# Sparse experts after delta attention and a dense mixture: nine tiles in the first list in place of six, the second list in three pieces

## The chip, the core and the metric

The program runs on one core of one Trainium2 chip. The metric is the device time of one execution in microseconds (us). A core has a matrix engine (TensorE, PE; its weight loads are listed as PEld), three elementwise engines (VectorE, DVE; ScalarE, ACT; GpSimd, POOL) and a queue that only issues transfers (SyncE, SP). Each engine works through its own instruction list in order and waits for the others through semaphores; 16 DMA engines move the data.

## What is computed

Three stages, cut to what matters here:

```python
y   = delta_attention(q, k, v, beta)          # 4 x 8 heads, 768 steps, head_dim 48
x   = y as rows                               # N = 3072 rows, D = 384
x   = sum_e p[:, e] * (relu(x @ w1[e]) @ w2[e])      # dense, E = 4, F = 1024, weights moe_*
# sparse stage, E = 8, F = 1024, weights moe2_*
logits     = (x/|x|) @ (emb/|emb|).T / tau
expert_idx = argmax(logits, axis=1)
gate_w     = softmax(logits)[expert_idx]
for e in range(8):
    mask = expert_idx == e
    out[mask] = gate_w[mask, None] * (relu(x[mask] @ w1[e]) @ w2[e])
```

## The kernel before, in words

**First stage.** The 768 steps are cut into 12 blocks of 64; a block makes 256 rows. Attention for block s+1 runs beside the dense experts of block s, 32 places per block, and the order is written by hand in a table `at`. As soon as a block's dense rows are there, they are routed (`route_pieces`): the row is normalised, its expert is chosen, its place in that expert's list is counted (`rce` holds a running count per expert), the row goes to a DRAM buffer `xb` (L872) and its number to a DRAM table `ids` with 24 tiles of 128 entries for each expert (L873). Beside all that the eight sparse experts' weights are split into pairs of 16-bit halves and written to DRAM as `wimg`.

**Sparse stage.** It works on tiles of up to 128 rows of one expert, numbered here from 0. For each tile POOL gathers the rows from `xb` into `g` (`gather`, L1009, four buffers), SP turns them into `xt` with a transposing transfer (`turn`, L1030), SP loads the expert's weights into one of three slots (`weights`, L1024, four transfers; tile n uses slot n % 3), PE does 72 matmuls for the hidden layer (L1052) and 24 for the output (L1069), ACT and DVE split the hidden layer (L1056, L1057), ACT scales (L1073) and POOL scatters the result (L1074). The loop issues, for tile j: `gather(j + 3)`, `turn(j + 2)`, the tile itself in four steps (hidden 0, hidden 1, output 0, output 1), then `weights(j + 3)`. The four weight transfers are issued with a condition: from tile 3 on they move nothing when tile n has the expert of tile n - 3, since the slot then holds it.

**Lists.** Which expert and which rows a tile has is worked out on the chip. `list_a` (DVE) finds the number of tiles per expert and, for each place of the list, the expert and the row of the table `ids`; it ends with a gather on POOL of these rows into `lsi` (L956). `list_b` turns them with two small matmuls on PE (L965, L966) and makes the row numbers `idx`, the experts `ei` and the flags for the conditional loads. The first list is made while block 11 is still in the dense stage, from the counts of blocks 0 to 10, and takes the first `NA` full tiles in the order of the experts; the second is made after block 11 is routed and takes the rest. `NB = 2 * NS + 7 - NA` places are kept for it. Inside a list the tiles stand in order of the expert, that row is cut into three stretches of about equal length, and place p takes entry p // 3 of stretch p % 3, so that one slot stays with one stretch.

**Order around the change.** While the first tiles run, the last block is routed. `behind` holds what is issued after step 4 * j + n of the tiles: pieces of `route_pieces` at 0, 1, 2, 3, 5, 6, then `list_a(1)` at 7 (after tile 1) and `list_b(1)` at 11 (after tile 2). Tiles 0 to NT - 5 (27 tiles, NT = NA + NB = 31) always run; four more run under two conditions on the number of tiles.

Of the kernel before, what the change touches and what calls it, by code (L numbers as in the profile page):

```python
# [645 lines left out]
class Sparse:  # L646
# [249 lines left out]
        return o  # L896

    def list_a(self, ph):
        nc, rp, cp = self.nc, self.tp, self.tp
        NA = self.NA  # L900
        J = NA if ph == 0 else self.NB
        c = rp.tile([128, 8], F32, name=f"cnt{ph}")
        nc.vector.tensor_tensor(out=c, in0=self.rce, in1=self.e3k, op=ALU.subtract)
        if ph == 0:
            c1 = rp.tile([128, 8], F32, name="cnt1m")
            nc.vector.tensor_scalar(out=c1, in0=c, scalar1=-127.0, scalar2=None, op0=ALU.add)
            nt = self.tiles_of(c1, "ntA", ALU.is_gt, 0)
            cum = self.prefix(nt, "cumA")

            a = self.took = rp.tile([128, 8], F32, name="took")  # L910
            nc.vector.tensor_tensor(out=a, in0=nt, in1=cum, op=ALU.subtract)
            nc.vector.tensor_scalar(out=a, in0=a, scalar1=float(NA), scalar2=0.0, op0=ALU.add, op1=ALU.max)
            nc.vector.tensor_tensor(out=a, in0=a, in1=nt, op=ALU.min)
            nt, cum = a, self.prefix(a, "cumT")
        else:
            nt = self.tiles_of(c, "ntB", ALU.is_gt, 0)
            nc.vector.tensor_tensor(out=nt, in0=nt, in1=self.took, op=ALU.subtract)
            cum = self.prefix(nt, "cumB")


        w = rp.tile([128, 8], F32, name="lsw")
        e = self.lse = rp.tile([128, 1], F32, name="lse")
        k = rp.tile([128, 1], F32, name="lsk")
        l = rp.tile([128, 1], F32, name="lsl")
        sn = rp.tile([128, 2], F32, name="lsn")
        sw = rp.tile([128, 2, 11], F32, name="lsv")
        st, T = self.st, cum[:, 7:8]
        nc.vector.tensor_scalar(out=sw, in0=self.k3.rearrange("p (a b) -> p a b", a=2), scalar1=T, scalar2=None,
                                op0=ALU.is_lt)
        nc.vector.tensor_reduce(out=sn, in_=sw, axis=AX.X, op=ALU.add)  # L930
        nc.vector.scalar_tensor_tensor(out=l, in0=sn[:, 0:1], scalar=st[:, 1:2], in1=st[:, 0:1],
                                       op0=ALU.mult, op1=ALU.add)
        nc.vector.scalar_tensor_tensor(out=l, in0=sn[:, 1:2], scalar=st[:, 2:3], in1=l, op0=ALU.mult, op1=ALU.add)
        nc.vector.tensor_tensor(out=e, in0=self.pidx, in1=T, op=ALU.is_ge)
        nc.vector.scalar_tensor_tensor(out=l, in0=e, scalar=1000.0, in1=l, op0=ALU.mult, op1=ALU.add)
        nc.vector.tensor_scalar(out=w, in0=cum, scalar1=l, scalar2=None, op0=ALU.is_le)
        nc.vector.tensor_reduce(out=e, in_=w, axis=AX.X, op=ALU.add)
        nc.vector.tensor_tensor(out=w, in0=w, in1=nt, op=ALU.mult)
        nc.vector.tensor_reduce(out=k, in_=w, axis=AX.X, op=ALU.add)
        nc.vector.tensor_tensor(out=k, in0=l, in1=k, op=ALU.subtract)  # L940
        nc.vector.tensor_scalar(out=e, in0=e, scalar1=-8.0, scalar2=None, op0=ALU.add)
        if ph == 1:
            nc.vector.tensor_scalar(out=w, in0=self.em8, scalar1=e, scalar2=None, op0=ALU.is_equal)
            nc.vector.tensor_tensor(out=w, in0=w, in1=self.took, op=ALU.mult)
            r = rp.tile([128, 1], F32, name="lsr")
            nc.vector.tensor_reduce(out=r, in_=w, axis=AX.X, op=ALU.add)
            nc.vector.tensor_tensor(out=k, in0=k, in1=r, op=ALU.add)

        nc.vector.scalar_tensor_tensor(out=k, in0=e, scalar=24.0, in1=k, op0=ALU.mult, op1=ALU.add)
        nc.vector.tensor_scalar(out=k, in0=k, scalar1=192.0, scalar2=None, op0=ALU.add)  # L950
        nc.vector.tensor_scalar(out=w[:, 0:1], in0=e, scalar1=0.0, scalar2=1000.0, op0=ALU.is_ge, op1=ALU.mult)
        bi = rp.tile([128, 1], I32, name="lsb")
        nc.vector.tensor_tensor(out=bi, in0=k, in1=w[:, 0:1], op=ALU.max)
        ids = rp.tile([32, 128], F32, name="lsi")
        nc.vector.memset(ids, float(PAD))
        nc.gpsimd.indirect_dma_start(  # L956
            out=ids[0:J], out_offset=None, in_=self.ids,
            in_offset=bass.IndirectOffsetOnAxis(ap=bi[0:J], axis=0), bounds_check=191, oob_is_err=False)
        self.lst = (J, ids, e, cum)
# [120 lines left out]


@with_exitstack
def kernel(ctx, tc, q, k, v, beta, probs, w1, w2, emb, tau, v1, v2, out, NA=6):
    nc = tc.nc
    ctx.enter_context(tc.manual_schedule())
    NS = q.shape[2] // 64
# [4 lines left out]
    sparse = Sparse(ctx, tc, emb, tau, v1, v2, out, NS, ident, pp, NA)  # L1091
# [20 lines left out]
    second = {o: [g for p, g in steps[1][0] if p == o] for o in range(-8, 0)}  # L1112
# [31 lines left out]
    at = defaultdict(list)  # L1144
# [38 lines left out]
    lists, tiles, cols = {}, {}, {}  # L1183
# [27 lines left out]

    last = 32 * (NS - 1)
    at[last + 1].append(opened)
    at[last + 12].append(lambda: sparse.list_a(0))
    at[last + 18].append(phase_a)
    at[last + 30].append(lambda: columns(0))

# [21 lines left out]
    behind = defaultdict(list)  # L1239
    for o, g in zip((0, 1, 2, 3, 5, 6), pieces):  # L1240
        behind[o].append(g)
    behind[7].append(lambda: sparse.list_a(1))
    behind[11].append(lambda: lists.__setitem__("B", sparse.list_b(1)))

    def tile(j, ahead):
        C = cols.pop(j)
# [62 lines left out]
```

## Time and profile before

| what | value |
|---|---|
| three runs, median (lowest, highest) | 1208.43 us (1207.02, 1209.62) |
| the profiled execution, own time | 1208.76 us |
| its span | 1207.0 us |
| PE busy | 1134.7 us (94%) |
| DVE busy | 772.6 us (64%) |
| ACT busy | 636.6 us (53%) |
| POOL busy | 366.4 us (30%) |
| mean granted clock of PE | 0.973 |

Busy time is the time with an instruction of that engine running; waits are what is left. In the rows further down a window line gives, for a stretch in us from the span's start, the busy time of PE, PEld, DVE, ACT and POOL with the number of instructions, then PE's granted clock as a share of full speed (1.00 is 2.4 GHz, 0.50 is 1.2 GHz), the mean busy share of the 16 DMA engines and the GB/s they moved. A timeline line gives start, duration, engine, source line, operation, output<-input, and in brackets the idle time of the engine before it and what ended it.

### The profile page before, as it was taken

The numbers are of one execution on the slowest core, as the hardware profiler recorded it, in microseconds if no ns is written. First come the engines' busy times: TensorE is split into PE (matmuls) and PEld (weight loads), VectorE is DVE, ScalarE is ACT, GpSimd is POOL, SyncE is SP. The second block draws the span as 40 slices with busy tenths as digits, with TensorE's granted clock in tenths as the row PEclk, the third lists the DMA queues.
The fourth block names the chain that finished last, engine by engine and source line by source line (L and its number), as shares of the span: only waits on it lengthen the run. The fifth ranks groups of instructions, "written<-read, shape, count | busy, mean of one in ns | idle before, by whom it ended". The sixth has DMA issues, their size and how long they took to land. (4 is left out here: it accounts for less than half of the span.)

```text
span 1207.0 us, 34016 instructions
## 1 busy us (share of the span) xinstructions
PE 1134.7 (94%) x13738; PEld 891.1 (74%) x13738; DVE 772.6 (64%) x2818; ACT 636.6 (53%) x1167; POOL 366.4 (30%) x346
## 2 busy tenths in 40 slices
PE   2359899999999999999999999999999999999997
PEld 2337677778777777777777778777777777888776
DVE  8858668788687786877868778687863543211221
ACT  8668766565565655656566565665653141222222
POOL 4346533231322313232133322332411203222221
PEclk8579999999999999999999999999999999999999
DMA  9971155645836556364474554646421293978951
GB/s 175 214 160 41 28 93 132 120 93 133 113 100 121 90 133 113 100 121 91 133 106 132 122 118 132 106 133 120 106 80 28 71 323 88 354 197 261 319 144 30
DMA packets 246162, 159.17 MB, mean 132 GB/s; under 512 B 195231, under 2 KB 229356, under 8 KB 246000
## 3 DMA queue, kind: packets, MB, share of 16 engines
q1 hardware_dynamic: 241600, 147.26, 53.1%
q0 software_dynamic: 4400, 9.68, 2.6%
q8 instruction: 110, 1.80, 0.7%
q14 instruction: 52, 0.43, 0.2%
HBM read 142.53 MB, written 35.80 MB: 148 GB/s over the span
## 5 line engine op out<-in xcount | busy, mean ns | idle before, releaser
L621 PE MATMUL po<-W,H 128*128 128x384 f16 x2304 | 408.6, 327 | 11.6 <-DVE H L604 8.8
L599 PE MATMUL ph<-xT,W 128*128 128x256 f16 x3456 | 411.2, 274 | 0.2
L599 PEld LDWEIGHTS <-W 128*128 128x128 f16 x3456 | 333.3, 98 | 49.6 <-issue 0.7
L621 PEld LDWEIGHTS <-H 128*128 128x128 f16 x2304 | 220.2, 98 | 146.6 <-DVE H L604 14.5
L604 DVE SCALAR_TENSOR_TENSOR H<-ph,H 128x512 f16<-128x512 f32 x192 | 131.7, 687 | 181.6 <-ACT H L603 180.2
L603 ACT ACTIVATE H<-ph 128x512 f16<-128x512 f32 x192 | 113.7, 593 | 143.3 <-PE ph L599 142.1
L788 POOL TENSOR_TENSOR wso<-wst,wso 128x768 f16<-128x768 f32 x64 | 105.6, 1650 | 245.4 <-ACT wst L787 237.5
L1057 DVE SCALAR_TENSOR_TENSOR H<-ph,H 128x512 f16<-128x512 f32 x54 | 37.2, 690 | 152.7 <-ACT H L1056 152.7
L1052 PEld LDWEIGHTS <-slot 128*128 128x128 f16 x1944 | 112.3, 99 | 3.8 <-issue 0.5
L1052 PE MATMUL ph<-xt,slot 128*128 128x128 f16 x1944 | 114.7, 221 | 0.1
L334 DVE TENSOR_TENSOR tt<-tt,pr 128x60 f32<-128x60 f32 (+34 forms) x660 | 111.0, 210 | 0.7
L1069 PE MATMUL po<-slot,H 128*128 128x384 f16 x648 | 110.0, 326 | 0.6 <-DVE H L1057 0.6
L330 DVE TENSOR_TENSOR pr<-tt,KQ 128x60 f32<-128x60 f32 (+34 forms) x660 | 108.8, 203 | 0.8
L1069 PEld LDWEIGHTS <-H 128*128 128x128 f16 x648 | 62.1, 98 | 39.1 <-DVE H L1057 0.9
L1074 POOL DMA_INDIRECT out_dram<-ob,idx x27 | 27.4, 1013 | 168.4 <-ACT ob L1073 112.0
L786 ACT ACTIVATE wso<-wst 128x768 f16<-128x768 f32 x64 | 53.4, 835 | 42.5 <-issue 24.3
L1056 ACT ACTIVATE H<-ph 128x512 f16<-128x512 f32 x54 | 32.2, 597 | 79.3 <-PE ph L1052 76.4
L293 POOL TENSOR_TENSOR AO<-G,AO 32x256 f16<-32x256 f32 x48 | 32.7, 680 | 97.5 <-ACT AO L292 95.6
L873 POOL DMA_INDIRECT ids<-idt,si x24 | 24.7, 1028 | 118.8 <-DMA ids<-idt,si 60.0
L359 PEld LDWEIGHTS <-TB 128*128 128x128 f16 x1152 | 34.4, 98 | 35.5 <-ACT TB L351 27.7
L587 POOL TENSOR_TENSOR W<-W,W 128x768 f16<-128x768 f32 x29 | 47.7, 1654 | 37.7 <-ACT W L586 28.5
L1073 ACT ACTIVATE ob<-po,sm 128x384 f32<-128x384 f32 x27 | 15.7, 580 | 82.1 <-PE po L1069 82.0
(261 smaller groups left out, 1444.3 us busy)
## 6 DMA issues: line engine op xcount, KB each, us to landing
slot<-wimg SPq DMA_DIRECT2D x108, 768.0 KB
wst<-in_moe_w_dram SPq DMA_DIRECT2D x65, 384.0 KB
wimg<-wso SPq DMA_DIRECT2D x64, 384.0 KB
W<-in_moe_w_dram SPq DMA_DIRECT2D x15, 384.0 KB
xb<-xr SPq DMA_DIRECT2D x48, 98.0 KB
Kr<-in_k_dram SPq DMA_DIRECT2D x24, 192.0 KB
Qr<-in_q_dram SPq DMA_DIRECT2D x24, 192.0 KB
Vr<-in_v_dram SPq DMA_DIRECT2D x24, 192.0 KB
```

What stands on the lines that cost most here:

```text
L330: nc.vector.tensor_tensor(out=p, in0=t[:, :, j:j + 1].to_broadcast([128, m, j]), in1=AT[:, j, 0:j].unsqueeze(1).to_broadcast([128, m, j]), ...
L334: nc.vector.tensor_tensor(out=t, in0=t, in1=p, op=ALU.subtract)
L587: low.tensor_tensor(out=lo, in0=t, in1=hi, op=ALU.subtract)
L599: nc.tensor.matmul(ph[:, i], w1[:, a, k, 128 * i:128 * i + 128], xT[:, b, k], start=(n == 0), stop=(n == 8))
L603: nc.scalar.activation(out=H[:, 0], in_=ph, func=AF.Relu)
L604: nc.vector.scalar_tensor_tensor(out=H[:, 1], in0=ph, scalar=0.0, in1=H[:, 0], op0=ALU.max, op1=ALU.subtract)
L621: nc.tensor.matmul(po[t], H[:, a, i, 128 * t:128 * t + 128], w2[:, b, i], start=(f == 0 and i == 0 and n == 0), stop=(f == 3 and i == 1 an ...
L786: self.nc.scalar.activation(out=o[:, 0], in_=t, func=AF.Copy, scale=scale)
L788: self.nc.gpsimd.tensor_tensor(out=o[:, 1], in0=t, in1=o[:, 0], op=ALU.subtract)
L1052: nc.tensor.matmul(ph[:, i], w[:, a, k, 128 * (i % 2):128 * (i % 2) + 128], xt[:, 3 * b + k], start=(m == 0), stop=(m == 8))
L1057: nc.vector.scalar_tensor_tensor(out=H[:, 1], in0=ph, scalar=0.0, in1=H[:, 0], op0=ALU.max, op1=ALU.subtract)
L1069: nc.tensor.matmul(po, H[:, a, i], w[:, b, i % 2], start=(q == 0 and i == 0 and m == 0), stop=(q == 1 and i == 3 and m == 2))
```

## The change

The first list takes nine full tiles in place of six, so the second has 22 places in place of 25. `list_a` becomes a generator with two `yield`s; the first list still runs through it in one go, the second is made in three pieces, after steps 7, 9 and 11, and `list_b(1)` comes after step 18 in place of 11.

```diff
     def list_a(self, ph):
...
             nt = self.tiles_of(c, "ntB", ALU.is_gt, 0)
             nc.vector.tensor_tensor(out=nt, in0=nt, in1=self.took, op=ALU.subtract)
             cum = self.prefix(nt, "cumB")
+        yield
...
         nc.vector.tensor_tensor(out=k, in0=l, in1=k, op=ALU.subtract)
         nc.vector.tensor_scalar(out=e, in0=e, scalar1=-8.0, scalar2=None, op0=ALU.add)
+        yield
         if ph == 1:
...
-def tile_delta_attention__then__two_moes_kernel(ctx, tc, q, k, v, beta, probs, w1, w2, emb, tau, v1, v2, out, NA=6):
+def tile_delta_attention__then__two_moes_kernel(ctx, tc, q, k, v, beta, probs, w1, w2, emb, tau, v1, v2, out, NA=9):
...
-    at[last + 12].append(lambda: sparse.list_a(0))
+    at[last + 12].append(lambda: list(sparse.list_a(0)))
...
-    behind[7].append(lambda: sparse.list_a(1))
-    behind[11].append(lambda: lists.__setitem__("B", sparse.list_b(1)))
+    second = sparse.list_a(1)
+    for o in (7, 9, 11):
+        behind[o].append(lambda: next(second, None))
+    behind[18].append(lambda: lists.__setitem__("B", sparse.list_b(1)))
```

PE, around the two small matmuls of the second list (`lsi`, `lse`). Before, between the last output matmul of tile 2 and the first hidden one of tile 3:

```order
L1069 LDWEIGHTS H_17459
L1069 MATMUL po<-slot_3_16251,H_17459 128x384
L965 MATMUL ps<-id_16252,lsi 128x32
L966 MATMUL ps<-id_16252,lse 1x32
L1052 LDWEIGHTS slot_0_16240
L1052 MATMUL ph<-xt_17171,slot_0_16240 128x128
```

Now, between the two halves of tile 4's output:

```order
L1072 LDWEIGHTS H_17703
L1072 MATMUL po<-slot_1_16245,H_17703 128x384
L968 MATMUL ps<-id_16252,lsi 128x32
L969 MATMUL ps<-id_16252,lse 1x32
L1072 LDWEIGHTS H_17743
L1072 MATMUL po<-slot_2_16246,H_17743 128x384
```

They stand seven half tiles later in PE's list.

POOL, in the first tiles: `g` is a tile's gather, `out_dram` a tile's scatter, `lsi` the gather of the list. Before:

```order
L873 DMA ids<-idt,si 24576x1 x2
L1074 DMA out_dram<-ob,idx_16685 3072x384
L956 DMA lsi<-ids,lsb 25x128
L1009 DMA g_16256<-xb,idx_16685 128x392
L1074 DMA out_dram<-ob,idx_16685 3072x384
L1009 DMA g_16257<-xb,idx_17500 128x392
```

Now:

```order
L873 DMA ids<-idt,si 24576x1 x2
L1077 DMA out_dram<-ob,idx_16685 3072x384
L1012 DMA g_16256<-xb,idx_16685 128x392
L1077 DMA out_dram<-ob,idx_16685 3072x384
L959 DMA lsi<-ids,lsb 22x128
L1012 DMA g_16257<-xb,idx_16685 128x392
```

The gather of tile 5 and the scatter of tile 2 now stand ahead of the list's gather, and tile 6 takes its rows from the first list (`idx_16685`).

DVE, at the two cuts of the second list in the change (H is the hidden layer of a tile, two instructions a tile):

```order
L886 TENSOR_REDUCE cumB<-pfw 128x8
L1060 SCALAR_TENSOR_TENSOR H_17386<-ph,H_17386 128x512
L1060 SCALAR_TENSOR_TENSOR H_17426<-ph,H_17426 128x512
L930 TENSOR_SCALAR lsv<-k_221,cumB 128x22
...
L943 TENSOR_SCALAR lse<-lse 128x1
L1042 TENSOR_SCALAR sm<-sm 128x1
L1043 RECIPROCAL sm<-sm 128x1
L946 TENSOR_SCALAR lsw<-em_210,lse 128x8
```

Before, the 27 instructions from `cnt` to the clearing of `lsi` (L903 to L955) stood in one row ahead of both H instructions of tile 2.

## Rows read from the trace of the kernel before

**Rows 1.** Timeline of PE: the first hidden matmuls of tiles 1, 2, 4 and 5

```profile
989.13 4.18 PE L1052 MATMUL ph<-xt,slot 128*128 128x128 f16 x72
997.17 4.18 PE L1052 MATMUL ph<-xt,slot 128*128 128x128 f16 x72
...
1018.07 4.18 PE L1052 MATMUL ph<-xt,slot 128*128 128x128 f16 x72
...
1025.99 4.18 PE L1052 MATMUL ph<-xt,slot 128*128 128x128 f16 x72
```

**Rows 2.** Timeline of all engines from tile 2's output to tile 3

```profile
1001.57 1.21 DVE L1057 SCALAR_TENSOR_TENSOR H<-ph,H 128x512 f16<-128x512 f32 x2
...
1002.24 3.75 PE L1069 MATMUL po<-slot,H 128*128 128x384 f16 x22 [0.56 <-DVE H L1057]
...
1005.97 1.04 POOL L956 DMA_INDIRECT lsi<-ids,lsb  x1 [4.46 <-DMA slot<-wimg]
...
1008.35 0.24 PE L965 MATMUL ps<-id,lsi 32*128 32x32 f32 x1 [2.36 <-DMA lsi<-ids,lsb]
...
1008.56 5.78 PE L1052 MATMUL ph<-xt,slot 128*128 128x128 f16 x72
```

**Rows 3.** Windows: the stretch right behind that wait

```profile
1008.00:1012.00 4.00, 3.65 (x36) 3.58 (x37) 1.36 (x9) 0.00 (x0) 2.42 (x3) 0.57 0.49 118
```

**Rows 4.** DMA view from 985 us on: issues, size of one, of the weights

```profile
slot<-wimg SPq DMA_DIRECT2D x96, 768.0 KB
```

**Rows 5.** Timeline of SP: weight loads of tiles 0, 4, 7; turn of tile 7

```profile
960.17 2.24 SPq L1024 DMA_DIRECT2D slot<-wimg  x4
...
1000.58 1.48 SPq L1024 DMA_DIRECT2D slot<-wimg  x4
...
1023.26 3.26 SPq L1024 DMA_DIRECT2D slot<-wimg  x4
1026.63 1.44 SPq L1030 DMA_TRANSPOSE xt<-g  x1
```

**Rows 6.** Windows: starts of two loads, and the three transposes behind loads 7 to 9

```profile
962.00:962.50 0.50, 0.50 (x5) 0.30 (x4) 0.04 (x1) 0.00 (x0) 0.38 (x1) 1.00 0.86 307
...
1025.00:1025.50 0.50, 0.50 (x5) 0.29 (x3) 0.00 (x0) 0.00 (x0) 0.00 (x0) 1.00 0.83 270
...
1034.50:1035.00 0.50, 0.50 (x13) 0.50 (x11) 0.00 (x0) 0.19 (x1) 0.00 (x0) 1.00 1.29 65
1035.00:1035.50 0.50, 0.50 (x13) 0.50 (x11) 0.00 (x0) 0.00 (x0) 0.00 (x0) 1.00 0.06 19
...
1045.00:1045.50 0.50, 0.50 (x13) 0.50 (x11) 0.37 (x1) 0.00 (x0) 0.42 (x1) 1.00 1.49 61
...
1055.50:1056.00 0.50, 0.50 (x5) 0.29 (x3) 0.05 (x1) 0.00 (x0) 0.00 (x0) 1.00 2.52 34
1056.00:1056.50 0.50, 0.50 (x5) 0.29 (x3) 0.00 (x0) 0.00 (x0) 0.00 (x0) 1.00 0.06 25
```

**Rows 7.** Windows: start of load 16, and the transpose behind load 18

```profile
1097.00:1097.50 0.50, 0.50 (x5) 0.31 (x4) 0.00 (x0) 0.00 (x0) 0.00 (x0) 1.00 0.83 344
...
1126.50:1127.00 0.50, 0.50 (x5) 0.31 (x4) 0.47 (x3) 0.00 (x0) 0.07 (x1) 1.00 1.74 92
```

**Rows 8.** Windows: end of a transposing transfer in the first stage

```profile
390.75:391.00 0.25, 0.25 (x5) 0.23 (x3) 0.00 (x0) 0.00 (x0) 0.00 (x0) 1.00 3.51 95
```

**Rows 9.** Timeline of DVE: what waited for that transfer

```profile
391.16 0.76 DVE L249 TENSOR_TENSOR KQ<-KTB 128x512 f16<-128x512 f16 x2 [1.82 <-DMA KTB<-KB]
```

**Rows 10.** Windows: PE's idle time in block 0, with the clock

```profile
125.00:126.00 1.00, 0.52 (x4) 0.10 (x1) 0.97 (x2) 0.97 (x2) 0.00 (x0) 1.00 0.00 0
126.00:127.00 1.00, 0.22 (x2) 0.11 (x2) 0.97 (x2) 0.98 (x2) 0.00 (x0) 1.00 0.00 0
127.00:128.00 1.00, 0.73 (x22) 0.64 (x23) 0.61 (x2) 0.97 (x3) 0.00 (x0) 1.00 0.00 0
```

**Rows 11.** Windows: a load alone on the queue

```profile
1040.00:1044.00 4.00, 4.00 (x52) 3.24 (x50) 0.00 (x0) 0.58 (x1) 0.24 (x1) 1.00 1.03 418
```

More of the change, by code (lines that the diff above doesn't have):

```diff
@@ L1082, with kernel @@
 @with_exitstack
-def kernel(ctx, tc, q, k, v, beta, probs, w1, w2, emb, tau, v1, v2, out, NA=6):
+def kernel(ctx, tc, q, k, v, beta, probs, w1, w2, emb, tau, v1, v2, out, NA=9):
     nc = tc.nc
```

## The prediction

> **What bounds the kernel now.** I read the busy times first: PE has 1134.7 of 1207.0 us, so only PE's gaps and its clock can give time back. In the sparse stage the timeline of PE shows tiles that follow each other without a gap: tile 4 starts at 1018.07 and tile 5 at 1025.99, so an undisturbed tile costs 7.92 us [rows 1]. The stage's one large gap is where the second list is made [rows 2]: PE stands 0.56 us inside tile 2 because its H came late from DVE, which was busy with the list; then 2.36 us ahead of the list's small matmuls, which wait for `lsi`, issued by POOL at 1005.97. Behind that gap the windows give a clock of 0.57 between 1008 and 1012 us [rows 3], the lower level (1.2 GHz) for most of it, and tile 3's 72 hidden matmuls take 5.78 us in place of 4.18 [rows 1, 2]. In a last view, the windows in steps of half a us, I look at the DMA engines, because the change also alters which tiles share weights; there the reader is to see that a tile's transpose runs only when the load issued ahead of it has ended.
>
> **What goes: the list's gap.** The small matmuls now stand inside tile 4. POOL can issue `lsi` once tile 2 has been scattered, at about 1007.5; in the old order it took 1008.35 - 1005.97 = 2.4 us from issue to PE [rows 2], so it is there by 1010, and PE reaches the matmuls at about 1019: nine us of cover. The gap and the lost clock go: 2.36 + (5.78 - 4.18) = 3.96 us. The cut of the list puts both H instructions of tile 2 ahead of the second piece, so the 0.56 us goes too. Together **-4.52 us**. The 0.2 us of the small matmuls stays. What the list now delays: on POOL the gather of tile 6 stands behind `lsi`, on SP `turn(6)` waits for that gather; tile 6 starts at about 1029, some 20 us after, so this costs nothing. DVE's third piece stands ahead of tile 3's H, but runs while tile 3's hidden matmuls do. Three more columns in the first list's small instructions cost nothing either: DVE's list instructions work on one row there, and the list is not made later.
>
> **What comes: two more loads, in longer rows.** Counting the reference's choices for its inputs gives 631, 338, 180, 721, 242, 603, 98, 259 rows for experts 0 to 7, and 4, 2, 1, 5, 1, 4, 0, 1 full tiles after eleven blocks. Put through the list's rule, the tiles' experts are, with NA = 6: 0 0 1 0 0 1 | 0 3 5 1 3 5 2 3 5 2 4 6 3 4 7 3 5 7 3 5 7, and with NA = 9: 0 0 2 0 1 3 0 1 3 | 0 3 5 1 4 5 2 4 6 3 5 7 3 5 7 3 5 7. 27 tiles run in both. A load moves data when the expert differs from that three places earlier: before for tiles 0, 1, 2, 7, 8, 9, 12, 16, 17, 18, 20, 22; now for 0, 1, 2, **4, 5**, **10, 11, 12, 13**, 15, **17, 18, 19, 20**. The longest row behind the start grows from three to four, and there is a new pair at tiles 4 and 5, early.
>
> A load is 4 x 768 KB [rows 4]. The queue of SP works in order: tile 7's turn was issued at 1026.63 [rows 5] but the transpose's burst of DMA activity ends at 1035.0, right behind load 7; those of tiles 8 and 9 end at 1045.5 and 1056.0 [rows 6]. Load 7 began to flow at 1025.0, so a cycle (load, the other tiles' gather and scatter beside it, transpose, and the nearly empty half us after it) takes 10.0, 10.5, 10.5 us. The second row, loads 16 to 18, flows from 1097.0 and its last burst ends at 1127.0 [rows 7]: 30.0 / 3 = 10.0. Call the cycle c; it lies between **10.0 and 10.5**, I take 10.2, the mean of all six. A tile takes 7.92, so each load in a row makes the next `xt` 2.3 us later against PE, and a row that lasts long enough runs out of lead. From the end of a transpose's burst to a waiting engine I take 0.5 us: in the first stage a transpose's burst ended at about 391.0 and DVE, which waited for it, began at 391.16 [rows 8, 9]; 0.5 leaves room for the windows' half us.
>
> - **Tile 13** (and **tile 20**, the same): load 10 flows 6.9 us after tile 7's start (1025.0 - 1018.07 for load 7 and tile 4 [rows 1, 6]), so tile 13's `xt` is there 6.9 + 4c + 0.5 after it, and PE wants it after 6 x 7.92 = 47.5. Late by 4c - 40.1: nothing at c = 10.0, **0.7 us** at 10.2, 1.9 at 10.5. Tile 12's comes 38.0 after, wanted at 39.6: in time.
> - **Tile 5**: load 4's issue at 1000.58 [rows 5] stays, since it stands behind the routing of the last block; before, it moved nothing. A load flows 1.7 to 1.8 us after its issue (960.17 to 962.0, 1023.26 to 1025.0 [rows 5, 6]), so at 1002.4; tile 5's `xt` is there at 1002.4 + 2c + 0.5 = 1023.3. PE without the old gap ends tile 2 at 1005.43 (1002.24 + 3.75 - 0.56), then two tiles and 0.2: 1021.5. **1.8 us** late; 1.4 at c = 10.0, 2.4 at 10.5. Tile 4's `xt`, at 1013.1, is wanted at 1013.35: in time.
>
> The clock after these new gaps is not in the trace. From below, 1.53 us idle within three us of block 0 left it at 1.00 [rows 10]; from above, 2.36 us in one piece lost it for 1.60 us of PE time [rows 2, 3]. 1.8 is nearer to 1.53, 0.7 far below: I charge nothing, and keep 1.6 us per gap for the upper end.
>
> Sum: -4.52 + 1.8 + 0.7 + 0.7 = **-1.3 us**. Against the profiled execution's own time of 1208.76 that is 1207.5; that execution lies 0.33 us above the median of the runs, so 1208.43 - 1.3 = **1207.1**. A measurement of this kernel can tell about 0.2%, 2.4 us, from no change: my forecast is no change that can be told.
>
> **Rivals.** (a) *The queue keeps up.* With c at 10.0 or under, tiles 13 and 20 wait for nothing and tile 5 for 1.4 us or less: -3.1, or 1205.3; with c under 9.3 tile 5 waits for nothing either: -4.5, or 1203.9. For it: the second row of three did run at 10.0, and a load alone moves 418 GB/s [rows 11], which is 7.5 us for its bytes. Against it: the emptier half us behind each transpose [rows 6], and 10.5 twice. The Trainium skill (DMA: Bandwidth & Descriptors, section Bandwidth) gives 436 GB/s as the ceiling and, in the section Latency and other measured facts, 261 GB/s for a DMA transpose; as an estimate from that page a cycle would be 3.54 MB / 436 + 0.2 MB / 261 = 8.9 us, no gap would be left at tiles 5, 13 and 20, and the time would be 1203.9. The trace's 10.0 to 10.5 disagrees, and the measurement decides the sum.
>
> (b) *The new gaps cost the clock.* At c = 10.5 tile 5's gap is 2.4 us, as long as the old one, and takes 1.6 us of clock with it, at the very place that was to be cured; tiles 13 and 20 wait 1.9 each. -4.5 + 2.4 + 1.6 + 3.8 = +3.3: 1211.7, and 1214.9 if those two lose the clock as well. It decides from a gap of about 2 us on. For it: two of three cycles in the first row, and a 2.36 us gap that did lose it. Against it: the mean cycle is shorter.
>
> (c) *The small matmuls wait again*, at their new place: only if `lsi` came nine us late; I give it no chance of its own.
>
> **How the numbers follow.** Forecast 0.41, (a) 0.33, (b) 0.26. The forecast's own span, 1205.5 to 1210.5, lies nearly all within 0.2%; (a) counts as faster but for a little at its edge, (b) as slower but for a little. So faster 0.35, same 0.40, slower 0.25. The range takes (a) whole and (b) up to where a second gap loses the clock: 1203.8 to 1213.0.
>
> **What would show it.** Right: no idle time of PE ahead of the two small matmuls, none inside tile 2, tile 3's 72 matmuls in 4.18 us; PE idle just ahead of the first hidden matmul of tile 5 (about 1.8 us), 13 and 20 (under 1 us each), each with a transpose's burst ending half a us earlier; a clock of 1.00 through the stage. Wrong: no gap at tile 5 (then (a)), a clock of 0.5 behind one of the gaps (then (b)), a gap at other tiles, or loads for other tiles than those listed.

## The result and the profile after

The changed kernel takes **1226.67 us** (median of 4 runs, 1222.40 to 1228.22) where the kernel before takes 1209.03 on the same chip (4 runs): a ratio of **1.0143, interval 1.0123 to 1.0163**. It is slower by some 17.6 us, where no change that can be told was forecast, and it lies outside the range. The profiled execution has a span of 1226.4 us against 1207.0.

The timeline of PE in the changed kernel, first hidden matmuls (L1055) of tiles 1, 2, 3, 4, then the list's two small matmuls, then tiles 5, 6, 11, 12, 13 and 20. The columns are start, duration, engine, line, operation, tiles; in brackets how long PE stood before it and for what.

```profile
988.69 4.18 PE L1055 MATMUL ph<-xt,slot 128*128 128x128 f16 x72
996.93 4.18 PE L1055 MATMUL ph<-xt,slot 128*128 128x128 f16 x72
1004.85 4.18 PE L1055 MATMUL ph<-xt,slot 128*128 128x128 f16 x72
1018.64 5.69 PE L1055 MATMUL ph<-xt,slot 128*128 128x128 f16 x72 [5.71 <-DMA xt<-g]
1026.21 0.24 PE L968 MATMUL ps<-id,lsi 32*128 32x32 f32 x1
1026.30 0.19 PE L969 MATMUL ps<-id,lse 32*1 32x32 f32 x1
1030.17 4.18 PE L1055 MATMUL ph<-xt,slot 128*128 128x128 f16 x72 [1.62 <-DMA xt<-g]
1038.10 4.35 PE L1055 MATMUL ph<-xt,slot 128*128 128x128 f16 x72
...
1078.47 4.18 PE L1055 MATMUL ph<-xt,slot 128*128 128x128 f16 x72
...
1087.72 4.18 PE L1055 MATMUL ph<-xt,slot 128*128 128x128 f16 x72 [0.71 <-DMA xt<-g]
...
1099.62 5.81 PE L1055 MATMUL ph<-xt,slot 128*128 128x128 f16 x72 [3.47 <-DMA xt<-g]
...
1162.19 5.60 PE L1055 MATMUL ph<-xt,slot 128*128 128x128 f16 x72 [4.83 <-DMA xt<-g]
```

What the change was made of has come: no idle time stands ahead of the small matmuls at 1026.21, tile 3 runs its 72 matmuls in 4.18 us, and PE's two idle times of [rows 2] are gone. In their place PE waits for `xt` at five tiles. The waits of PE from 975 us on (total, times, longest):

```profile
PE ph L1055 <- DMA xt<-g: 16.3, 5, 5.7
PE po L1072 <- DVE sm L1042: 0.6, 3, 0.2
```

The tally against before: -4.52 us for the list's gap, +16.34 for the five waits (5.71 + 1.62 + 0.71 + 3.47 + 4.83), +0.6 for `sm`, and +4.56 for the clock at tiles 4, 13 and 20 (5.69 + 5.81 + 5.60 in place of 3 x 4.18). That is 17.0 of the 19.4 us between the spans; the rest is spread, for instance tiles 5 to 11 begin 48.30 / 6 = 8.05 us apart in place of 7.92. The forecast had three waits of 3.2 us in sum and nothing for the clock. The list of loads in the prediction is confirmed by the bytes: two loads more are 2 x 4 x 786,432 bytes = 6.29 MB, and the pages of before and after read

```profile
DMA packets 246162, 159.17 MB, mean 132 GB/s; under 512 B 195231, under 2 KB 229356, under 8 KB 246000
```

```profile
DMA packets 247314, 165.46 MB, mean 135 GB/s; under 512 B 195352, under 2 KB 229488, under 8 KB 247152
```

Now the places that answer to [rows 5] and [rows 6]. SP's timeline, the issue of load 4 and of tile 4's transpose:

```profile
1000.75 3.80 SPq L1027 DMA_DIRECT2D slot<-wimg  x4
1004.59 3.71 SPq L1033 DMA_TRANSPOSE xt<-g  x1
```

Windows of the changed kernel: the start of load 4, the transposes behind loads 4 and 11 and, in full, behind load 12, and the 4 us behind tile 13's start. The columns are the stretch, its length, busy time of PE, PEld, DVE, ACT and POOL, the granted clock, the DMA share and GB/s.

```profile
1006.50:1007.00 0.50, 0.50 (x13) 0.50 (x11) 0.10 (x1) 0.00 (x0) 0.50 (x1) 1.00 0.35 49
1007.00:1007.50 0.50, 0.50 (x13) 0.50 (x11) 0.00 (x0) 0.02 (x1) 0.18 (x1) 1.00 0.82 307
...
1015.50:1016.00 0.50, 0.00 (x0) 0.00 (x0) 0.00 (x0) 0.00 (x0) 0.50 (x1) 0.50 3.82 125
...
1073.50:1074.00 0.50, 0.50 (x13) 0.50 (x10) 0.47 (x1) 0.00 (x0) 0.20 (x2) 1.00 4.43 169
...
1084.50:1085.00 0.50, 0.48 (x3) 0.09 (x2) 0.50 (x1) 0.12 (x2) 0.00 (x0) 1.00 3.60 104
1085.00:1085.50 0.50, 0.29 (x2) 0.21 (x3) 0.38 (x3) 0.00 (x0) 0.00 (x0) 1.00 0.09 37
1085.50:1086.00 0.50, 0.50 (x5) 0.29 (x3) 0.00 (x0) 0.00 (x0) 0.00 (x0) 1.00 0.05 10
1086.00:1086.50 0.50, 0.50 (x5) 0.29 (x3) 0.00 (x0) 0.00 (x0) 0.00 (x0) 1.00 1.07 325
...
1087.50:1088.00 0.50, 0.28 (x6) 0.31 (x7) 0.00 (x0) 0.12 (x1) 0.00 (x0) 1.00 1.04 424
...
1095.50:1096.00 0.50, 0.50 (x5) 0.20 (x2) 0.00 (x0) 0.00 (x0) 0.00 (x0) 1.00 3.38 270
...
1100.00:1104.00 4.00, 4.00 (x46) 4.00 (x44) 0.36 (x1) 0.60 (x1) 1.28 (x2) 0.57 1.01 408
```

The reader is to see three things. Load 4 was issued at 1000.75, but flows only from 1007.0 (by the packet records its first packets begin at 1002.7 and are held for up to 4.3 us each; see the last section). The burst behind load 12 (share 3.60, few GB/s) ends at 1085.0, and tile 12 starts at 1087.72, 2.7 us later; behind load 4 it is 1016.0 and 1018.64, behind load 13 1096.0 and 1099.62. And after the burst behind load 12 the DMA engines stand nearly still for a us (0.09, 0.05), with load 13 already on the queue; in the half us after 1016.0 and 1096.0 the share was 0.34 and 0.67.

The trace's records of single DMA packets tell why the burst is not the end. Packets of SP's queue that began in each half us, behind load 12:

```
half us from   256-byte packets (transpose)   6144-byte packets (loads)
1083.5                    0                           38
1084.0                  348                            1
1084.5                  155                            2
1085.0                    0                            3
1085.5                   20                            0
1086.0                  239                           15
1086.5                    6                           16
1087.0                    0                           10
1087.5                    0                           26
```

The transpose of a tile is 768 packets of 256 bytes (128 x 6 x 256 = 196,608 bytes) and moves here in two parts, some 500 and some 260, with 1 to 1.5 us of pause between them. The burst is the first part. The next load begins to move only with the second. This shape belongs to the place in a row and not to the transpose: by the same records those of tiles 4, 6 and 11 of the kernel before, with no load moving ahead of them, ran whole in 1.1 us, where those of tiles 7, 8 and 9 took 2.4 to 2.8 us.

### The profile page after: what moved, and what is told of

It reads as the page before. It is cut to its first block, busy times and chain, and to the rows that moved or that the text cites. A ratio compares the mean times of both kernels' runs of the same rounds, so it can differ in the third digit from the quotient of the medians.

```text
span 1226.4 us, 34016 instructions
## 1 busy us (share of the span) xinstructions
PE 1140.2 (93%) x13738; PEld 893.4 (73%) x13738; DVE 774.3 (63%) x2818; ACT 636.9 (52%) x1167; POOL 367.1 (30%) x346
## 5 line engine op out<-in xcount | busy, mean ns | idle before, releaser
L1055 PE MATMUL ph<-xt,slot 128*128 128x128 f16 x1944 | 118.2, 223 | 16.4 <-DMA xt<-g 16.3
L1055 PEld LDWEIGHTS <-slot 128*128 128x128 f16 x1944 | 115.2, 100 | 21.3 <-issue 18.1
```

The source lines that it names most:

```text
L1055: nc.tensor.matmul(ph[:, i], w[:, a, k, 128 * (i % 2):128 * (i % 2) + 128], xt[:, 3 * b + k], start=(m == 0), stop=(m == 8))
```

## The experiments

Fourteen kernels, each timed beside the kernel before on its chip. The medians of the kernel before there:

| experiments | before, us |
|---|---|
| nine tiles in the old places; six in the new; nine without the later loads; transpose ahead of its load | 1210.05 |
| a row of four; the gather a tile earlier; ScalarE's queue; without scatters | 1209.09 |
| rows cut; without the transposes of the rows; the first of the last four | 1208.63 |
| the second, third and last of the last four | 1208.17, 1212.77, 1211.24 |

The ratio to before and its 95% interval are those on record for the runs; they lie up to 0.2% from the quotient of the two medians. Theory A: a transpose stands behind its tile's load on SP's queue, and the list of nine puts loads in rows. Theory B: the new places of the list's pieces make the waits. Theories C and D put it on the loads' bytes, or on gathers and scatters.

### Nine tiles, old places

```
- tile_delta_attention__then__two_moes_kernel(..., NA=6):
+ tile_delta_attention__then__two_moes_kernel(..., NA=9):     # the rest as before
```

> Only the size of the first list is changed (nine), the second list's pieces stay where the kernel before has them. Theory A (a tile's DMA transpose stands behind that tile's weight load in SP's queue, and the list of nine puts the loads in rows of two and four): TensorE waits for xt at tiles 4, 5, 12, 13 and 20 as in the changed kernel (16.3 us in 5 waits there), and the list gap ahead of tile 3 is back, so 1226.4 + 2 to 4.5 = 1228 to 1231 us. Theory B (the new places of the list's pieces, which move work of VectorE, GpSimd and the ids' gather, make the waits): about the kernel before, 1207 to 1211 us.

Measured 1226.37 us, 1.0150 (1.0117 to 1.0184). The waits of PE:

```profile
PE ph L1052 <- DMA xt<-g: 9.4, 3, 4.5
PE ps L965 <- DMA lsi<-ids,lsb: 6.7, 1, 6.7
PE po L1069 <- DVE H L1057: 0.7, 1, 0.7
```

The size alone makes the kernel as slow as the changed one, and a little less slow than the 1228 to 1231 expected. The three `xt` waits stand at tiles 12, 13 and 20 (1.59, 3.34, 4.46); at tiles 4 and 5, against the expectation, there is none: PE stood 6.7 us for the list just before. Part of this loss is thus the list's, whose `lsi`, issued at 1006.02, let PE go on at 1011.43, 5.4 us later in place of 2.4; load 4 flowed beside it. That load 4 is the reason is not shown.

### Six tiles, new places

```
  NA=6
- behind[7]: list_a(1), whole             + behind[7], [8], [9]: its three pieces
```

> Six tiles in the first list as before, and the second list in three pieces at places 7, 8 and 9 with its small matmuls at 11 as before. Theory A: no new wait for xt, 1205 to 1210 us, at most the 0.56 us wait of the second matmuls changes. Theory B: waits for xt appear, 1215 us or more.

Measured 1210.35 us, 1.0008 (0.9989 to 1.0027). The waits view has one line for PE, the list's 3.9 us, and none for `xt`: theory B falls, though the time lies 0.35 us above theory A's span.

### Nine tiles without the later loads

```
- kw = dict(cond=cv > 0, cond_hint=False)
+ kw = dict(cond=cv > 1, cond_hint=False)     # never true; from tile 3 on no weights come
```

> The changed kernel with the condition of every weight load behind the first three never true: it leaves out the weights of the tiles from the fourth on, so that what remains is the gain of the change with no load in the way. Theory A: no wait for xt of over 0.5 us, all tiles at 7.92 to 8.1 us, and the kernel before less the list gap, its clock and the H wait: 1209.0 - 4.5 = 1203 to 1206 us. Theory B: the waits stay, 1220 us or more.

Measured 1204.67 us, 0.9958 (0.9941 to 0.9974): 5.1 us less than before, and PE waits for nothing in the whole stage. The gain of 4.5 us is real; the loads take it back.

### Rows cut

```
+ kw = dict(cond=cv > (1 if n in (4, 12, 19) else 0), cond_hint=False)
```

> The changed kernel with the loads of places 4, 12 and 19 left out (their tiles use the weights that lie in the slot): eight loads behind the first three remain, the longest row is two (10, 11 and 17, 18). Theory A (rows): no wait for xt of over 0.5 us is left and the clock stays, 1203 to 1207 us. Rival (each load costs something wherever it stands, 20 us over eleven loads): eight of them cost about 14 us, 1216 us or more.

Measured 1204.49 us, 0.9963 (0.9947 to 0.9978), and again no wait of PE. Eight loads leave the gain whole, eleven cost 22 us more. At one price a load the eight would have cost about 14 us, so what counts is which loads follow one another. It also shows that load 5 alone, with no load 4 ahead, is in time.

### A row of four in the kernel before

```
- if n >= 3:
+ if n >= 3 and n != 10:          # NA=6; load 10 runs unconditionally
```

> The kernel before with one load more: place 10 is loaded whether its expert differs or not, which makes the row 7, 8, 9 a row of four and changes nothing else. Theory A: xt waits at tile 10 by 2.5 to 4 us, about 1.5 us of clock with it, and tile 9 waits 0.3 us as before: ratio 1.003 to 1.005, 1213 to 1216 us where before is 1210. Theory E (the row is harmless, and the waits of the changed kernel come from its list's other order of tiles or from load 4): within 1 us of before.

PE's timeline at tile 10:

```profile
1070.35 5.81 PE L1052 MATMUL ph<-xt,slot 128*128 128x128 f16 x72 [3.77 <-DMA xt<-g]
```

3.77 us of wait (theory A's upper end is 4) and 5.81 - 4.18 = 1.63 of clock, in a list that is otherwise the old one; at tile 9 PE's record shows no wait. The trace is for theory A. The times do not settle it: 1213.61 us, 1.0017 (0.9991 to 1.0044), runs from 1208.34 to 1215.25.

### The transpose ahead of its load

```
-     if j + 2 < sure: turn(j + 2)
      tile(j, sure)
      if j + 3 < sure:
+         turn(j + 3)
          weights(j + 3)
```

> The changed kernel with one line moved: each tile's transpose is issued ahead of that tile's weight load and not behind it (the first three likewise). Theory A: the waits for xt (16.3 us and 4.6 us of clock) are gone, 1204 to 1208 us, unless a load is now late. Theory C (two more loads of 3.1 MB and their rows are too much for the DMA engines, whichever goes first): TensorE waits for the slots' weights in place of xt, 1215 to 1228 us.

Measured 1220.57 us, 1.0081 (1.0044 to 1.0118). PE's waits, SP's longest wait between 1005 and 1018 us, and its timeline at load 5:

```profile
PE ph L1055 <- DMA slot<-wimg: 13.0, 15, 2.3
```

```profile
SPq L1033 <- DMA g<-xb,idx: 9.2, 1, 9.2
```

```profile
1014.51 1.29 SPq L1033 DMA_TRANSPOSE xt<-g  x1
1017.59 1.67 SPq L1027 DMA_DIRECT2D slot<-wimg  x2
```

Every wait for `xt` is gone, tile 4 starts without any, and now the loads are late (theory C's sign). One reason is in the other two fences: SP stood at tile 5's transpose for 9.2 us until its gather had landed, and issued load 5 another 3.1 us later, 11.6 us after tile 2 had left the slot at 1006.0.

### The same with the gather a tile earlier

```
-     if j + 3 < sure: gather(j + 3)
+     if j + 4 < sure: gather(j + 4)
```

> As the run with the transpose ahead of the load, and each tile's gather one tile earlier, so that SP's queue does not stand at a transpose that waits for its gather (there turn 5 waited until 1014.51 and load 5 was issued at 1017.59 in place of about 1007). Theory A (order on SP's queue is what costs): tile 5 in time, and the last of a row of four late by the cycle alone, 4 x 10 us against 39.6: 0 to 3 us at tiles 13 and 20 each; 1205 to 1212 us. Theory D (the gathers and scatters, which run between and beside the loads, slow each load whatever the order is): waits for slots of 10 us or more stay, 1215 to 1221 us.

Measured 1216.27 us, 1.0055 (1.0032 to 1.0079): the time lies in theory D's span, and the waits for slots are just under its 10 us.

```profile
PE ph L1055 <- DMA slot<-wimg: 9.6, 10, 2.0
```

Tiles 4 and 5 wait 2.1 us each for their weights, so tile 5 is not in time, though theory A had it so. The longest wait is at tile 13, inside its hidden matmuls; the 18 behind it, 1.18 us at full clock, show the clock's fall:

```profile
1095.26 2.10 PE L1055 MATMUL ph<-xt,slot 128*128 128x128 f16 x18 [1.96 <-DMA slot<-wimg]
```

### Transposes on ScalarE's queue

```
- self.nc.sync.dma_start_transpose(...)
+ self.nc.scalar.dma_start_transpose(...)
```

> The changed kernel with the tiles' transposes issued by ScalarE in place of SP, so that they stand in another queue than the loads. Theory A: waits for xt of over 1 us are gone, and the loads follow each other without a transpose between them; 1204 to 1210 us. Theory D (transposes, gathers and loads share the DMA engines, and order in one queue is not what delays them): xt still waits 10 us or more in sum, 1218 us or more.

Measured 1270.52 us, 1.0491 (1.0431 to 1.0550): as theory D has it, and worse. ScalarE's timeline (tile 10's transpose, tile 11's, and the H behind that), then PE's at tile 10:

```profile
1064.67 1.52 ACTq L1033 DMA_TRANSPOSE xt<-g  x1
...
1080.21 1.23 ACTq L1033 DMA_TRANSPOSE xt<-g  x1
1081.54 0.60 ACT L1059 ACTIVATE H<-ph 128x512 f16<-128x512 f32 x1 [8.45 <-issue]
```

```profile
1091.58 5.81 PE L1055 MATMUL ph<-xt,slot 128*128 128x128 f16 x72 [3.40 <-DMA xt<-g]
```

Tile 10's transpose was issued at 1064.67 and ended the wait at 1091.58, 26.9 us later, though no load stood ahead of it in its queue; in the changed kernel tile 12's, behind its load, took from 1073.05 to 1087.72, 14.7 us. And ScalarE, which stood at a transpose whose gather was late (tile 11's gather, issued at 1066.76, let it go on at 1080.21), kept PE waiting for H for 23.3 us in sum. So "behind the load on the same queue" is not the whole mechanism: beside loads that are under way, in a queue of its own, this transpose fared worse. The Trainium skill says that spreading DMAs over SP, ACT and GpSimd does not help bandwidth, since they all run on the same 16 DMA engines (DMA: Bandwidth & Descriptors, section Rules for kernel authors); the trace agrees that there is no gain, and shows a loss besides, 26.9 us against 14.7.

### Without scatters

```
  ob = ...; nc.scalar.activation(out=ob, in_=po, ...)
- nc.gpsimd.indirect_dma_start(out=self.out, ...)      # tiles 1 to 20
```

> The changed kernel without the scatter of the output of tiles 1 to 20 (their rows of the output are left out). Theory A: the loads' cycle is set by load and transpose, so the waits for xt stay within 3 us of 16.3 in sum, 1222 us or more. Theory D: the scatters, which share the DMA engines and GpSimd's queue with the gathers, are a large part of the delay: the waits fall under 10 us, 1216 us or less.

Measured 1219.46 us, 1.0089 (1.0065 to 1.0113), between the two again.

```profile
PE ph L1055 <- DMA xt<-g: 12.2, 4, 6.4
```

Tile 13 waits 2.09 us in place of 3.47, tile 20 2.21 in place of 4.83, tiles 5 and 12 not at all; tile 4 waits 6.38, and tile 19, which had not waited, 1.55. The scatters are a part of the cycle: without them the waits are a quarter shorter, and tiles 13 and 20 keep the clock.

### Without the transposes of the rows

```
+ if n in (5, 11, 12, 13, 18, 19, 20): return (*T, self.xt)    # the xt of the tile before
  xt = self.xt = self.t2.tile(...)
```

> The changed kernel with the transposes of tiles 5, 11 to 13 and 18 to 20 left out (they compute with the xt of the tile before), so that the rows are loads alone with their gathers and scatters. Theory A1 (the transposes in a row both wait and hold the load behind them): the load cycle falls from 10 to about 8.5 us, waits for slots at tiles 12, 13, 20 under 1 us each; tile 4 waits as before (5.7 us and clock), 1212 to 1216 us. Theory C (3.1 MB a tile with gather and scatter is too much): the cycle stays at 10 us and slots wait 2 us or more at tiles 13 and 20, 1218 us or more.

Measured 1211.74 us, 1.0014 (0.9993 to 1.0035). PE waits once, 5.1 us at tile 4. A window over loads 11 to 13:

```profile
1061.50:1087.00 25.50, 25.50 (x323) 20.85 (x321) 5.51 (x13) 6.49 (x16) 7.66 (x8) 1.00 1.02 410
```

The loads with their gathers and scatters flow at 410 GB/s without a break; by the packet records loads 12 and 13 begin 8.4 and 8.5 us after the one before. No slot is late: theory C falls for rows of four without transposes. With a transpose in each cycle the bursts of the changed kernel end at 1063.0, 1074.0, 1085.0 and 1096.0: 11.0 us.

### A version with the gain and without the loss

Of the next four kernels three keep six tiles in the first list, hence the old loads, and take the list off PE's front by making its small matmuls in tile 3 and gathering tile 6 late. The last kernel goes back to nine.

```
  NA=6; list_a(1) in pieces at 7, 9, 10
+ behind[14]: list_b(1)
+ in tile j == 4: gather(6) ahead of gather(7)
```

> Six tiles in the first list, so the loads of the kernel before, but the second list in pieces at 7, 9 and 10, its small matmuls at 14 and the gather of tile 6 one tile later, so that nothing of the list stands at TensorE's front. Theory A (the gain is the list gap with its clock and the H wait; the loss is rows of loads): all of the gain, none of the loss: 1203 to 1206 us where before is 1209, ratio 0.995 to 0.997. Rival: turn 6 now waits on SP for its late gather and holds load 7 behind it: a wait of 1 to 4 us at tile 7, ratio 0.998 or more.

Measured 1211.39 us, 1.0018 (1.0004 to 1.0033). The list's gap is gone, but PE waits 4.09 us at tile 8 and 3.70 at tile 9: the rival, though at the row's later tiles and not at tile 7. The next run takes the cause away that its expectation names.

```
+ list_a(1) in pieces at 7, 8, 9; behind[14]: list_b(1), then gather(6)
```

> As the run with the small matmuls at 14, but the second list's pieces at 7, 8 and 9 and the gather of tile 6 issued directly behind its list and not with the next tile. In that run turn 6 stood on SP until 1019.15 for its gather, and load 7 came at 1022.28 though its slot came free from about 1018.8. Theory A (the row 7, 8, 9 then starts with its slot, and keeps the margin that it had before): waits of at most 0.5 us at tiles 8 and 9, 1203 to 1206 us, ratio 0.995 to 0.997. Rival (the margin of the row came from the list gap itself): waits of 2 us or more at tiles 8 and 9 stay, ratio 0.999 or more.

Measured 1207.51 us, 0.9990 (0.9969 to 1.0011): no change that can be told, and half of the rival. Tile 8 is in time, tile 9 still waits 3.43 us and loses the clock:

```profile
1056.65 5.81 PE L1055 MATMUL ph<-xt,slot 128*128 128x128 f16 x72 [3.43 <-DMA xt<-g]
```

So now the order is turned as well:

```
+ behind[14]: list_b(1), gather(6), gather(7);  gather(j + 4) at the head of tile j
- turn(j + 2) ahead of tile(j)
+ in weights(j + 3): the two register loads, then turn(j + 3), then the four DMAs
+ at the start: gather(0) to gather(3), and turn(2) ahead of weights(1)
```

> As the run with the gather of tile 6 behind its list, and each tile's transpose ahead of its own load, with the gathers one tile earlier. Theory A (order is what costs; a row of three loads by itself is in time): the wait of 3.43 us and 1.63 us of clock at tile 9 go, at most 1 us of waits for slots comes, 1203 to 1206 us, ratio 0.995 to 0.997. Theory C (a load needs 10 us or more where a tile takes 7.92, whatever the order): waits for slots of 2 us or more at tile 9, ratio 0.998 or more.

Measured **1208.18 us where before is 1212.77: 0.9956 (0.9936 to 0.9977)**, faster than the kernel before, where the changed one is slower. PE's waits:

```profile
PE ph L1057 <- issue: 0.8, 2, 0.5
PE po L1074 <- DVE H L1062: 0.2, 1, 0.2
PE po L1074 <- ACT H L1061: 0.2, 1, 0.2
```

SP's timeline at load 7:

```profile
1019.40 1.23 SPq L1035 DMA_TRANSPOSE xt<-g  x1
1021.02 2.54 SPq L1029 DMA_DIRECT2D slot<-wimg  x4
```

Load 7 is issued 1.6 us after its transpose, and the whole row 7, 8, 9 runs without a wait. Order, earlier gathers and earlier register loads came in one step here; what each is worth with six tiles is not separated.

The same order with nine tiles:

> Nine tiles in the first list as in the changed kernel, transposes ahead of the loads, gathers one tile earlier, and the registers of a load read ahead of the transpose, so that the load follows it at once. Theory A (order and issue are what costs): every load starts 1.5 to 3 us sooner, waits for slots fall from 9.6 to 0 to 5 us; 1204 to 1211 us where before is 1209. Theory C (rows of four are too much for the DMA engines, whatever the order): 7 us or more of waits for slots stay, 1213 us or more.

Measured 1213.34 us where before is 1211.24, 1.0019 (1.0003 to 1.0035).

```profile
PE ph L1057 <- DMA slot<-wimg: 6.7, 7, 1.9
```

The time lies in theory C's span, the waits of 6.7 us between the two expectations. The row 10 to 13 no longer waits; 3.1 us stand at tiles 4 and 5 and 3.6 at tiles 19 and 20. The cycle itself did not get shorter than the forecast's 10.2: by the packet records the row's loads begin at 1047.2, 1058.4, 1069.1 and 1079.8. What the order changes is that `xt` no longer comes behind the tile's own load, whose four parts PE waits for one by one. With the best order tried the list of nine still gives back its gain.

## Why the prediction was wrong, step by step

- **The list's gap, -4.52: right.** 2.36 + 1.60 + 0.56 are gone, and the two runs whose loads do not get in the way are 0.42 and 0.37% faster than before, 5.1 and 4.5 us.
- **The loads and the rows: right.** The tiles named are those that load; the bytes agree, and the waits stand at 5, 13 and 20 as forecast, and at 4 and 12, which were called in time.
- **"From the end of a transpose's burst to a waiting engine I take 0.5 us": this step failed.** Measured 2.6 at tile 4, 2.7 at 12, 3.6 at 13, and by windows of the same kind 2.7 at 5 and over 4 at 20. The burst of [rows 6] is the first of two parts. The packets of the kernel before show the same for tile 9: the first part to 1056.0, the second from 1056.5 to 1057.5, and PE started that tile at 1057.98. And the burst of [rows 8] was not KTB's: by the packet records the 2 x 2048 packets of the two KTB transposes (524,288 bytes each) had all begun by 388.0, and those from 390.0 on belong to the transposes of QT, issued at 388.99. DVE [rows 9] came 3.2 us after the last packet of what it waited for; I had matched it with another transfer. This step is in all five waits: it brings `xt` 2.1 to 3.7 us later than forecast, more than the whole wait of 1.62 at tile 5 and of 0.71 at tile 12.
- **"A load flows 1.7 to 1.8 us after its issue, so at 1002.4": failed for load 4.** It flowed from 1007.0, 4.6 us later: its first packet began at 1002.7, as forecast, but the first packets were held. This makes up most of the waits at tiles 4 and 5: tile 4's `xt` was forecast for 1013.1 and came at 1018.64 (4.6 late start, 2.1 second part, less 1.2 for a cycle of 9.0). The two loads that gave 1.7 and 1.8 had no routing just ahead of them; this one stands right behind that of the last block. What held its packets stays open (last section).
- **The cycle of 10.2: too short.** From 1053.5, where load 10 begins to flow, to the fourth burst's end at 1096.0 it is 42.5 / 4 = 10.6; burst to burst 11.0. For tile 13: 0.4 later start, 4 x 0.4 = 1.7 for the cycle and 3.1 for the second part are 5.2 us, of which PE, itself delayed by then, felt 3.47 where 0.7 was forecast.
- **The clock, charged nothing: right by the row, wrong in sum.** The gaps of 1.62 and 0.71 left it at 1.00; those of 5.71, 3.47 and 4.83 cost 1.51, 1.63 and 1.42 us, as rival (b) had it for longer gaps. Its bound of about 2 us is not borne out as one: 2.21 us kept the clock in one run, and 1.96 lost it in another (last section).
- **Rival (a)** asked for a cycle of 10.0 or under and fell by the 10.6, and the first step would have undone it at 10.0 too. The Trainium skill's 261 GB/s for a DMA transpose (DMA: Bandwidth & Descriptors, section Latency and other measured facts) makes 0.75 us of 0.197 MB, as an estimate; the traces have 1.1 us for a transpose with no load ahead, and 2.4 to 3.5 us from first packet to last for those behind a load at tiles 7 to 9 before and 4, 11, 12 and 13 now.

What had to be seen in the trace before: the half us after the burst, named in the rival as "emptier", was the pause inside the transpose, and tile 9's start 0.3 us late was the wait itself.

## What to carry to other kernels

Where a small transfer that the next tile needs first and a large one that it needs piece by piece stand on one queue, the order on that queue matters beside the bytes: the transpose first, the load's registers read before it, and its source gathered early enough that the queue never stands at it. With nine tiles these steps took the ratio from 1.0143 to 1.0081, 1.0055 and 1.0019; without the later loads it is 0.9958, so bytes and rows keep the rest. Ask of a change that moves work into a quiet place what else its parameter sets, here which tiles share weights, and give a row of back-to-back loads the price of a whole cycle with everything that interrupts it. And follow a transfer to its last packet before a latency is taken from it.

## What the runs showed of the hardware

- In a row of loads a DMA transpose of 196,608 bytes moves as about 500 and 260 packets of 256 bytes with 1 to 1.5 us between them, and the load behind it on the queue moves only with the second part: 11.0 us from burst to burst with it, 8.4 and 8.5 from load to load without. With no load ahead three of the kernel before ran whole in 1.1 us.
- Issued from another engine's queue beside loads, the same transpose took 26.9 us from issue to use, against 14.7 behind its load on SP's queue.
- The first 16 or so packets of load 4, 6144 bytes each, took up to 4.3 us apiece in the changed kernel (most of them 2.6 to 4.3, begun from 1002.7 to 1003.7), where other packets of loads take 0.24. By the packet records of all eight runs with a load 4 the hold goes with the last block's second write to `ids`. Where the load began within 0.2 us of that write's packets (the changed kernel, the old places, without scatters, without the rows' transposes, ScalarE's queue), the slowest took 3.8 to 4.8 us. It took 2.4 us where 1.7 us lay between (nine tiles with the last order), 1.1 us where 3.5 us lay between (the early gather), and 1.4 us where the load went ahead of the write (the transpose ahead). But in these three a transpose ran just ahead of the load as well, and no run moves the write alone: that it is the cause is not shown.
- PE's clock after an idle stretch: 2.21 us (the run without scatters) left tile 20's 72 matmuls at 4.18, with a granted clock of 1.00, and 2.23 us (the transpose ahead of the load) left 18 matmuls at 1.18. In that same run 2.33 us was followed by 2.10 us for 18 matmuls, at 0.50, and in the run with the early gather so was 1.96 us, with 0.69 us idle and 1.18 us of work just ahead of it. The length of one idle stretch does not settle it.
